# A later place for four key casts, and a third queue for seven stores, in a fused attention and GELU kernel

## The chip, the cores and the metric

The kernel runs on one core of one Trainium2 chip. The metric is the device time of one execution in microseconds (us); several executions are timed and the median counts. Engines are named as the profile names them: PE multiplies matrices (PEld loads its weights), DVE and ACT work on vectors, POOL (GpSimd) does too and issues DMAs, SP only issues DMAs; ACT can issue them as well.

## What is computed

The reference is sliding-window attention, window 32 to either side, for 8 batches, 8 heads, 576 positions and 64 elements a head, followed by a two-layer feed-forward with the tanh form of GELU on the 4608 rows that come out of it:

```python
scores = scale * np.matmul(q, k.transpose(0, 1, 3, 2))
mask = np.abs(pos[:, None] - pos[None, :]) <= window
attn = exp(where(mask, scores, -1e9) - max) / sum
x = (attn @ v).transpose(0, 2, 1, 3).reshape(4608, 512)
h = x @ w_in                        # 512 -> 2048
g = 0.5 * h * (1.0 + np.tanh(c * (h + 0.044715 * h * h * h)))
out = g @ w_out                     # 2048 -> 512
```

Inputs and output are float32.

## The kernel before

The 4608 rows are cut into nine tiles of 512 (t = 0 to 8; `NT` is 9). While the feed-forward of tile t runs on PE, the attention of batch b = t + 1 is worked in between its matmuls, and the raw data of batch t + 2 is loaded and cast. The heads of a batch go in pairs (g = 0 to 3), and the last positions of all pairs make a fifth group (g = 4). A group is scored on PE (`score`), exponentiated on ACT, masked on DVE (`mask`, line 511), summed by a matmul with ones (`sum_up`, line 516), weighed with V on PE (`times`, line 526), inverted on ACT (`invert`, lines 553 and 554) and written to the next rows on DVE (`spread`, line 563).

The order of instructions on each engine is the order of the program text; nothing reorders it. The last part of a tile is a loop over 112 steps, each with one product matmul of the output layer (`ffn_out`, line 774, its matmul on line 793). Before step i, everything that a plan lists under i is put out. A plan is a table from step to acts: `s` scores a group, `m` masks it, `g` sums and weighs a pair of groups, `x` spreads one, `a` casts a quarter of the next batch's queries (`turn_query`, cast on line 431), `b` casts a quarter of its keys (`turn_keys`, cast on line 441). The last query quarter issues a transposing DMA on SP (line 435), and every second key quarter issues one (line 443). Tiles 4 to 6 use `PLAN`, tile 3 `PLAN_L`; line 1024 chooses:

```python
PLAN = {7: "s0@0 s1@1 v-1", 16: "m0 m1 x-1", 35: "s2@0 g0@1", 38: "m2", 46: "x0 a0", 52: "x1 a1 a2 a3",
        63: "s3@0 s4@1", 66: "b0 b1", 70: "m3", 74: "m4", 80: "b2 b3", 88: "g2@1", 108: "x2", 112: "x3"}
```

The keys that `turn_keys` casts come from four DMAs a batch, issued by `load_qk` (line 204) on SP at the front of the same tile, after two transposing DMAs on SP (lines 426 and 451).

The output layer is a Strassen-like scheme of seven products (`WINO`, n = 0 to 6), 16 matmuls each. After each product's last matmul, in steps 15, 31, 47, 63, 79, 95 and in `ffn_last`, DVE (or ACT) copies or adds the result: line 816 after step 63, line 819 after step 79 (822 in the last tile), line 825 after step 95, line 834 at the end of the tile. The result tile is `yo`, and `store` (line 746) writes its rows to the output. A store of 128 rows is cut into pieces where the rows of the output are not contiguous, and the pieces go round the queues that the caller names; without any, they go to POOL's queue. The last tile names queues, as its stores end the program: SP for the left half of the first 256 rows, then SP and ACT in turn. DMAs of SP and ACT share eight semaphores in rotation, and an issue waits until the store that had its semaphore before has landed. At the end of the program (shown as line 1170 in the profile) every engine drains, SP waits for all semaphores of DMAs, and all engines meet at POOL.

Of the kernel before, what the change touches and what calls it, by code (L numbers as in the profile page):

```python
# [36 lines left out]
def cut(b):  # L37
    return 120 if b else 128
# [7 lines left out]
PLAN = {7: "s0@0 s1@1 v-1", 16: "m0 m1 x-1", 35: "s2@0 g0@1", 38: "m2", 46: "x0 a0", 52: "x1 a1 a2 a3",  # L46
        63: "s3@0 s4@1", 66: "b0 b1", 70: "m3", 74: "m4", 80: "b2 b3", 88: "g2@1", 108: "x2", 112: "x3"}
# [5 lines left out]
PLAN_0 = {4: "s0@0", 9: "r1@1", 14: "s1@0", 15: "w1", 16: "m0", 19: "k2", 22: "r2@1", 23: "m1", 28: "s2@0 w2",  # L53
# [15 lines left out]
PLAN_2 = {7: "s0@0 s1@1 v-1", 16: "m0 m1 x-1", 35: "s2@0 g0@1", 38: "m2", 46: "x0", 52: "x1",  # L69
          63: "s3@0 s4@1", 66: "a0 a1", 70: "m3", 74: "m4", 80: "a2 a3", 88: "g2@1", 108: "x2", 112: "x3"}  # L70

PLAN_L = {7: "s0@0 s1@1 v-1", 16: "m0 m1 x-1", 35: "s2@0 g0@1", 38: "m2", 46: "x0", 52: "x1",
          63: "s3@0 s4@1", 66: "a0 a1", 70: "m3", 74: "m4", 80: "a2 a3", 84: "b0", 88: "g2@1", 92: "b1", 95: "b2 b3", 108: "x2", 112: "x3"}

PLAN_1 = {12: "s0@0 s1@1 s2", 16: "m0 m1", 36: "m2", 56: "s-1@0 g0@1", 62: "m-1 x0", 64: "x1",
          80: "s3@0 g-1@1", 81: "m3", 90: "x2", 92: "x-1", 104: "v3 s4@1", 112: "x3 m4"}
# [6 lines left out]
LONE = 3  # L83
# [5 lines left out]
def kernel(  # L89
# [9 lines left out]
    nc = tc.nc  # L99
    B, H, S, D = q.shape  # L100
# [304 lines left out]
    def bank(i):  # L405

        return psM.tile([128, 512], FP32, name="mm", tag=f"x{i}")
# [206 lines left out]
    def in_w(eng, unit, *which):  # L614

        i, j = UNITS[unit] // 2, 2 * (UNITS[unit] % 2)
        A11, A12, A21, A22 = (w_cols[:, d:d + 2, c + i, j:j + 2, :] for c in (0, 2) for d in (0, 2))
        if (unit, "s") not in mixed:
            if unit == "A":
                wc = rawp.tile([128, 4, 2, 2, 128], FP16, name="wcA", tag="q0")  # L620
                mixed[unit, "s"] = [wc[:, x] for x in range(4)]
            else:
                mixed["xw"] = rawp.tile([128, 2, 4, 2, 256], FP16, name="xw", tag="k1")
                mixed[unit, "s"] = [mixed["xw"][:, 1, x].rearrange("p d (h c) -> p d h c", h=2) for x in range(4)]
        S1, S2, S3, S4 = mixed[unit, "s"]
        mixed[unit, "w"] = dict(A11=A11, A12=A12, A22=A22, S1=S1, S2=S2, S3=S3, S4=S4)
        for x in which:
            dst, a, b, op = ((S1, A21, A22, ALU.add), (S2, S1, A11, ALU.subtract),
                             (S3, A11, A21, ALU.subtract), (S4, A12, S2, ALU.subtract))[x - 1]
            eng.tensor_tensor(dst, a, b, op=op)  # L630
# [102 lines left out]
    def sums(t, i, which=slice(0, 4)):  # L733

        g, r = gTs[t], slice(2 * i, 2 * i + 2)
        A11, A21, A12, A22 = (g[:, r0 + 2 * i:r0 + 2 * i + 2, c:c + 256]
                              for r0 in (0, 8) for c in (0, 256))
        S1, S2, S3, S4 = (wino[f"S{n}"][:, r, :] for n in (1, 2, 3, 4))
        for dst, x, y, op in ((S1, A21, A22, ALU.add), (S2, S1, A11, ALU.subtract),
                              (S3, A11, A21, ALU.subtract), (S4, A12, S2, ALU.subtract))[which]:  # L740
            nc.vector.tensor_tensor(dst, x, y, op=op)  # L741
# [4 lines left out]
    def store(t, t4, yo, cols=slice(0, 512), *engs):  # L746

        m = i = 0
        while m < 128:
            b, c = divmod(t * 512 + t4 * 128 + m, S)  # L750
            q0, n = (0, cut(b)) if c < 4 * cut(b) else (cut(b), 144 - cut(b))
            j, p = divmod(c - 4 * q0, n)
            e = min(n - p, 128 - m)
            eng = engs[i % len(engs)] if engs else nc.gpsimd
            eng.dma_start(out_v[b, j, q0 + p:q0 + p + e, cols], yo[m:m + e, cols])  # L755
            m += e
            i += 1
# [16 lines left out]
    def ffn_out(t, i):  # L774

        n, blk, f = i // 16, i // 8 % 2, i % 8
        if n == 1 and t >= NT - 2:
            blk, f = divmod(i % 16, 4) if i % 16 < 8 else (i // 2 % 2, i // 4 % 4 * 2 + i % 2)
        a, w, new = WINO[n]
        end = t == NT - 1  # L780
        if i % 16 == 0 and new:
            pys[n % 2] = bank((1 + n) % 2)
            if end and n == 4:
                pys["apart"] = psO.tile([128, 512], FP32, name="py2", tag="O")
        py = pys[n % 2].rearrange("p (b c) -> p b c", b=2)
        apart = end and blk and n in (4, 6)
        if a[0] == "A":
            r0, c0 = 8 * (int(a[2]) - 1) + f, 256 * (int(a[1]) - 1) + 128 * blk
            lhsT = gTs[t][:, r0, c0:c0 + 128]
        else:  # L790
            lhsT = wino[a][:, f, 128 * blk:128 * blk + 128]
        one = end and n in (4, 6)
        nc.tensor.matmul(pys["apart"][:, 0:256] if apart else py[:, blk, :], lhsT,  # L793
                         wino[w][:, f, :], start=(new and i % (8 if one else 16) == 0),
                         stop=(i % (8 if one else 16) == (7 if one else 15)),
                         skip_group_check=True)
        if i % 16 < 15:
            return
        yo, left, right = wino["yo"], slice(0, 256), slice(256, 512)
        C11, C12, C21, C22 = (yo[:, r:r + 2, c] for r in (0, 2) for c in (left, right))  # L800

        M1, U2, U3 = C21, C12, C22
        if n == 0:
            (nc.scalar.copy if t >= NT - 2 else nc.vector.tensor_copy)(M1, py)
        elif n == 1:
            nc.vector.tensor_tensor(U2, py, M1, op=ALU.add)  # L806
        elif n == 2:
            nc.vector.tensor_copy(C11, py)
            if t >= NT - 2:
                for step in "z1 z2 z3".split():  # L810
                    sums(t, int(step[1]), PARTS[step[0]])
            if end:
                for x in range(2):
                    store(t, x, yo[:, x, :], left, nc.sync)
        elif n == 3:
            nc.vector.tensor_tensor(U3, py, M1, op=ALU.add)
        elif n == 4:
            if not end:
                nc.vector.tensor_tensor(C22, py, U3, op=ALU.add)
            else:  # L820
                for x, part in enumerate((py[:, 0, :], pys["apart"][:, 0:256])):
                    nc.vector.tensor_tensor(C22[:, x, :], part, U3[:, x, :], op=ALU.add)
                    store(t, 2 + x, yo[:, 2 + x, :], right, nc.sync, nc.scalar)
        elif n == 5:
            nc.vector.tensor_tensor(C21, py, M1, op=ALU.add)  # L825
            for x in range(2):
                store(t, 2 + x, yo[:, 2 + x, :], *((left, nc.sync, nc.scalar) if end else ()))

    def ffn_last(t):
        py = pys[0].rearrange("p (b c) -> p b c", b=2)  # L830
# [75 lines left out]
    s0 = psS.tile([128, 2, 512], FP32, name="ps_o", tag="S0")  # L906
# [4 lines left out]
    s1 = psS.tile([128, 2, 512], FP32, name="ps_o", tag="S1")  # L911
# [63 lines left out]
    for t in range(NT):  # L975
        b = t + 1
        att = b < B
        if t:
# [19 lines left out]
            for fc in range(begun, NF if t < LONE else 0):  # L998
# [22 lines left out]
                    pair_v(b, nc.vector.tensor_copy)  # L1021
                if t == LONE - 1 and fc in (8, 9, 10, 11):
                    in_w(nc.vector, "B", (8, 9, 10, 11).index(fc) + 1)
        plan = PLAN_0 if not t else PLAN_1 if t == 1 else PLAN_2 if t == LONE - 1 else PLAN_L if t == LONE else PLAN if att else {16: "v-1", 40: "x-1"} if t == B - 1 else {}

        def group(g):
            return (b, g) if g >= 0 else (b - 1, 4)
# [6 lines left out]
        for i in range(113 if t else 65):  # L1034
# [100 lines left out]
            if t == 0 and i < 64:  # L1135
                ffn_out_0(*ORDER_0[i])
            elif t and i < 112:
                ffn_out(t, i if t < NT - 1 or not 28 <= i < 36 else i + 4 if i < 32 else i - 4)
# [36 lines left out]
```

## Time and profile before

| what | value |
|---|---|
| timed executions | 292.73, 292.84, 294.62 us; median 292.84 |
| the profiled execution's own time | 293.94 us |
| its span, first to last instruction | 292.2 us |
| PE busy | 283.3 us, 97% |
| DVE, ACT, POOL busy | 77%, 67%, 32% |
| granted TensorE clock | 1.00 |
| tile 3, tile 4, tile 5, tile 6 (by PE's first matmul of each) | 30.22, 30.99, 29.88, 29.89 us |

The profile is one execution. Its own time is about 1.7 us more than its span, which is what lies before the first and after the last instruction. A line of the timeline gives start, duration, engine, line, operation, output and inputs with shapes, and in brackets how long the engine stood idle before and what ended that. In the table of stages each engine has its busy time and its number of instructions, and the last columns are the granted clock, the share of the DMA engines and GB/s. Landing times of DMAs are read from the semaphore updates that the trace holds.

### The profile page before, as it was taken

What the parts mean: (1) busy time and instruction counts of PE and PEld (TensorE: products, weight loads), DVE (VectorE), ACT (ScalarE), POOL (GpSimd) and SP (SyncE); (2) the same over time, 40 slices, a digit from 0 to 9 for tenths busy, and PEclk for the clock granted to TensorE, in tenths of its full rate; (3) what the DMA queues carried; (4) which work ended last, traced back from release to release, by engine and by line L of the source; (5) the groups of instructions that cost most, each with busy time, mean ns of one, the idle gap of its engine ahead of it and who ended that gap; (6) DMA issues with size and microseconds to landing.
All of it is one profiled execution on the core that took longest, in us unless ns stands there. A gap on an engine that the chain in (4) does not pass through costs nothing.

```text
span 292.2 us, 7443 instructions
## 1 busy us (share of the span) xinstructions
PE 283.3 (97%) x2993; PEld 197.0 (67%) x2993; DVE 225.5 (77%) x499; ACT 196.9 (67%) x323; POOL 92.7 (32%) x158
## 2 busy tenths in 40 slices
PE   8889999999999999999999989999999999999994
PEld 3535544557765677668866876688667877887783
DVE  4755377998897968798998778889888967875682
ACT  5875867878577865687658845895689577905800
POOL 3435324102318652505166108500800070016000
PEclk9999999999999999999999999999999999999999
DMA  7999998999999999869999998698820031005013
GB/s 219 276 372 399 358 311 201 246 195 187 272 222 195 261 217 192 220 156 217 134 185 248 179 162 185 193 180 126 186 45 2 2 87 61 0 3 144 0 43 103
DMA packets 113792, 51.01 MB, mean 175 GB/s; under 512 B 97839, under 2 KB 109615, under 8 KB 113502
## 3 DMA queue, kind: packets, MB, share of 16 engines
q1 hardware_dynamic: 89604, 38.77, 59.0%
q0 software_dynamic: 23088, 10.82, 23.1%
q10 hardware_dynamic: 1066, 0.96, 1.0%
q8 instruction: 23, 0.38, 0.6%
q14 instruction: 11, 0.09, 0.1%
HBM read 36.70 MB, written 9.44 MB: 158 GB/s over the span
## 4 chain that ended last, share of the span: by engine, by line
PE 82%; DMA 9%; SPq 5%; issue 1%; DVE 1%; POOL 0%; ACTq 0%; DVEq 0%
PE mm L793 29%; PE ph L600 17%; PE mm L600 14%; PE pu L656 7%; DMA kr<-in_k_dram 3%; PE ps_s L489 3%; PE py L765 3%; PE mm L765 2%; DMA wst<-in_moe_w_in_dram 2%; SPq L204 2%; DMA qr<-in_q_dram 2%; DMA V<-in_v_dram 1%; PE ps_od L516 1%; SPq L282 1%; PE ps_d L516 1%
## 5 line engine op out<-in xcount | busy, mean ns | idle before, releaser
L600 PEld LDWEIGHTS <-w_in 128*128 128x128 f16 x448 | 50.2, 113 | 39.6 <-POOL w_in L261 1.2
L755 POOL DMA_DIRECT2D out_dram<-y x77 | 42.0, 554 | 93.2 <-DVE y L825 75.3
L600 PE MATMUL ph<-xT,w_in 128*128 128x512 f16 x240 | 60.4, 379 | 0.6 <-POOL w_in L261 0.6
L793 PEld LDWEIGHTS <-s 128*128 128x128 f16 x512 | 49.4, 98 | 6.6 <-issue 0.4
L600 PE MATMUL mm<-xT,w_in 128*128 128x512 f16 x208 | 53.5, 379 | 0.0
L793 PE MATMUL mm<-t,s 128*128 128x256 f16 x376 | 44.9, 273 | 0.2 <-DVE y L806 0.2
L793 PEld LDWEIGHTS <-gT 128*128 128x128 f16 x384 | 36.2, 98 | 6.6 <-issue 0.3
L502 ACT ACTIVATE pe<-ps_s 128x960 f16<-128x960 f32 (+1 forms) x31 | 29.5, 974 | 14.2 <-PE ps_s L489 14.1
L793 PE MATMUL mm<-w_out,gT 128*128 128x256 f16 x256 | 32.6, 273 | 0.0
L741 DVE TENSOR_TENSOR s<-gT 128x512 f16<-128x512 f16 x64 | 26.9, 425 | 5.7 <-ACT gT L608 2.9
L608 ACT ACTIVATE gT<-mm 128x512 f16<-128x512 f32 x28 | 16.5, 599 | 21.6 <-PE mm L600 21.5
L608 ACT ACTIVATE gT<-ph 128x512 f16<-128x512 f32 x38 | 20.9, 606 | 6.6 <-PE ph L600 6.6
L114 ACT ACT_TABLE_LOAD x18 | 23.1, 1283 | 2.2 <-issue 1.9
L554 ACT ACTIVATE lt<-lt 128x480 f32<-128x480 f32 (+3 forms) x36 | 21.1, 585 | 1.1
L511 DVE TENSOR_TENSOR pe<-pe,band 128x960 f16<-128x960 f16 x28 | 18.1, 664 | 2.0 <-ACT pe L502 1.9
L704 ACT ACTIVATE gT<-ph 128x512 f16<-128x512 f32 x22 | 13.2, 600 | 4.8 <-PE ph L600 4.7
L793 PE MATMUL mm<-t,gT 128*128 128x256 f16 x128 | 16.2, 273 | 0.0
L526 PEld LDWEIGHTS <-V 128*64 128x64 f16 x520 | 12.6, 112 | 5.2 <-DVE V L237 1.3
L741 DVE TENSOR_TENSOR s<-s,gT 128x512 f16<-128x512 f16 x32 | 14.4, 450 | 1.1
L553 ACT ACTIVATE lt<-ps_od 128x480 f32<-128x480 f32 (+2 forms) x13 | 7.1, 546 | 11.6 <-PE ps_od L526 6.2
L793 PE MATMUL mm<-w_out,s 128*128 128x256 f16 x120 | 14.6, 273 | 0.0
L227 POOL DMA_DIRECT2D V<-in_v_dram x16 | 14.3, 912 | 0.5 <-PE mm L600 0.2
(153 smaller groups left out, 472.7 us busy)
## 6 DMA issues: line engine op xcount, KB each, us to landing
kr<-in_k_dram SPq DMA_DIRECT2D x31, 256.0 KB
qr<-in_q_dram SPq DMA_DIRECT2D x6, 1024.0 KB
wst<-in_moe_w_in_dram SPq DMA_DIRECT2D x8, 512.0 KB
vr<-in_v_dram SPq DMA_DIRECT2D x12, 256.0 KB
wst<-in_moe_w_out_dram SPq DMA_DIRECT2D x2, 1024.0 KB
wst<-in_moe_w_out_dram SPq DMA_DIRECT2D x4, 512.0 KB
V<-in_v_dram POOLq DMA_DIRECT2D x16, 128.0 KB, 8.2
qr<-in_q_dram SPq DMA_DIRECT2D x7, 256.0 KB
```

The costliest lines, as they stand in the source:

```text
L114: nc.scalar.add_instruction(mybir.InstLoadActFuncSet(name=nc.get_next_instruction_name(), act_func_set_id=which, ins=[], outs=[]))
L227: nc.gpsimd.dma_start(V[:, c, :, :], v[b, :, 128 * c:128 * c + 128, :].rearrange("h p d -> p h d"))
L502: nc.scalar.activation(pe, ps[:, :, 0:w], AF.Exp, scale=SCALE)
L511: nc.vector.tensor_tensor(pe, pe, m.rearrange("k (o j) p -> k o j p", o=1).broadcast_to(list(pe.shape)), op=ALU.mult)
L554: nc.scalar.activation(lt[:, 0:n], lt[:, 0:n], AF.Exp, scale=-1.0)
L600: nc.tensor.matmul(ph, w_cols[:, dc, fc // 4, fc % 4, :], xT[:, dc, t * 512 % RING:t * 512 % RING + 512], start=(dc == 0), stop=(dc == 3))
L608: nc.scalar.activation(gTs[t][:, fc, :], phs[fc], AF.Gelu_apprx_tanh)
L656: nc.tensor.matmul(ps[:, 256 * h:256 * h + 256], lhs[:, d, h, :], rhs[:, d, :], start=(n in (0, 2, 4) and h == d == 0), stop=(h == d == 1) ...
L741: nc.vector.tensor_tensor(dst, x, y, op=op)
L755: eng.dma_start(out_v[b, j, q0 + p:q0 + p + e, cols], yo[m:m + e, cols])
L765: nc.tensor.matmul(pys[t4], gTs[0][:, fc, t4 * 128:t4 * 128 + 128], w_out16[:, fc, :], start=new, stop=(fc == NF - 1))
L793: nc.tensor.matmul(pys["apart"][:, 0:256] if apart else py[:, blk, :], lhsT, wino[w][:, f, :], start=(new and i % (8 if one else 16) == 0) ...
```

## The change

Two edits. First, tile 4 (`LONE + 1`) gets a plan of its own, `PLAN_M`, in which the key casts b0, b1, b2 and b3 of batch 6 stand at steps 84, 92 and 95, after the masks m3 and m4 and after the addition that follows step 79; in `PLAN` they stand at 66 and 80. Everything else in the plan is the same. Second, in the last tile the stores that follow the addition after step 95 (line 825) go to other queues: the first 128 rows all to SP, the second 128 rows to ACT and POOL in turn; before, both went to SP and ACT in turn.

```diff
+PLAN_M = {7: "s0@0 s1@1 v-1", 16: "m0 m1 x-1", 35: "s2@0 g0@1", 38: "m2", 46: "x0 a0", 52: "x1 a1 a2 a3",
+          63: "s3@0 s4@1", 70: "m3", 74: "m4", 84: "b0", 88: "g2@1", 92: "b1", 95: "b2 b3", 108: "x2", 112: "x3"}
@@ ffn_out @@
         elif n == 5:
             nc.vector.tensor_tensor(C21, py, M1, op=ALU.add)
             for x in range(2):
-                store(t, 2 + x, yo[:, 2 + x, :], *((left, nc.sync, nc.scalar) if end else ()))
+                store(t, 2 + x, yo[:, 2 + x, :],
+                      *((left, *((nc.scalar, nc.gpsimd) if x else (nc.sync,))) if end else ()))
@@ the choice of the plan @@
-        plan = ... else PLAN_L if t == LONE else PLAN if att else ...
+        plan = ... else PLAN_L if t == LONE else PLAN_M if t == LONE + 1 else PLAN if att else ...
```

The pieces of the seven stores after line 825 were 40, 32, 24 and 24 rows on SP and 88, 24 and 24 on ACT; they are 40 and 88 on SP, 32, 24 and 24 on ACT and 24 and 24 on POOL.

More of the change, by code (lines that the diff above doesn't have):

```diff
@@ L1023 @@
                     in_w(nc.vector, "B", (8, 9, 10, 11).index(fc) + 1)
-        plan = PLAN_0 if not t else PLAN_1 if t == 1 else PLAN_2 if t == LONE - 1 else PLAN_L if t == LONE else PLAN if att else {16: "v-1", 40: "x-1"} if t == B - 1 else {}
+        plan = PLAN_0 if not t else PLAN_1 if t == 1 else PLAN_2 if t == LONE - 1 else PLAN_L if t == LONE else PLAN_M if t == LONE + 1 else PLAN if att else {16: "v-1", 40: "x-1"} if t == B - 1 else {}
         def group(g):
```

## The prediction

> **What bounds the kernel now.** I read the page's shares first: PE is busy 97% of the span at full granted clock, and the chain of work is 82% PE. So an edit pays only where PE stands still, or after its last matmul. Cutting the span into tiles, and tiles 4 and 5 at the same point of their own course (the score matmuls of groups 3 and 4, before step 63), gives four stages:
>
> ```profile
> 145.66:168.42 22.76, 22.76 (x230) 15.94 (x227) 19.49 (x46) 17.24 (x29) 10.79 (x17) 1.00 1.32 205
> 168.42:176.65 8.23, 7.33 (x115) 6.11 (x115) 6.75 (x17) 4.52 (x7) 0.73 (x2) 1.00 0.98 143
> 176.65:199.40 22.75, 22.75 (x229) 15.95 (x227) 19.34 (x44) 17.23 (x29) 9.95 (x16) 1.00 1.13 190
> 199.40:206.53 7.13, 7.13 (x115) 6.07 (x115) 6.52 (x15) 4.51 (x7) 0.73 (x2) 1.00 0.76 139
> ```
>
> Columns: window, its length, then PE, PEld, DVE, ACT and POOL busy. The first stages are equal (22.76 and 22.75 us). The second takes 8.23 us in tile 4 and 7.13 in tile 5, with the same 115 matmuls. So tile 4 loses 1.10 us there. The timeline shows how:
>
> ```profile
> 169.70 0.69 DVE L816 TENSOR_TENSOR y<-mm,y 128x512 f32<-128x512 f32 x1
> 171.68 0.76 DVE L441 CAST k<-kr 128x512 f16<-128x512 f32 x2 [1.30 <-DMA kr<-in_k_dram]
> 172.36 0.65 DVE L511 TENSOR_TENSOR pe<-pe,band 128x960 f16<-128x960 f16 x1
> 172.93 0.55 DVE L511 TENSOR_TENSOR pet<-pet,band 128x768 f16<-128x768 f16 x1
> 173.40 0.68 DVE L819 TENSOR_TENSOR y<-mm,y 128x512 f32<-128x512 f32 x1
> ...
> 171.77 0.39 PE L516 MATMUL ps_od<-pe,ones 128*64 128x480 f16 x2
> 173.06 0.39 PE L516 MATMUL ps_d<-pe,ones 128*64 128x480 f16 x2 [0.90 <-DVE pe L511]
> ```
>
> DVE works in order. At 170.38 it reaches batch 6's key casts (b0, b1), whose load lands at 171.56; it stands 1.30 us, the mask of group 3 comes that much late, and PE's denominator matmul waits 0.90 us for it. Tile 5 has the same order and no wait, because its last key load lands at 200.91 and its casts start at 201.15.
>
> At the end of the program I read the DMA queues and the shutdown (line 1170):
>
> ```profile
> 288.90 0.33 ACTq L755 DMA_DIRECT2D out_dram<-y  x1
> 289.26 0.32 SPq L755 DMA_DIRECT2D out_dram<-y  x1
> ...
> 261.98 5.77 POOL L755 DMA_DIRECT2D out_dram<-y  x11 [20.61 <-DVE y L825]
> L1170 POOLq DRAIN x3: 46/93/6027, 266.5 to 292.0; - x3
> L1170 SPq EVENT_SEMAPHORE  x11: 17/28/28, 289.6 to 292.2; - x11
> ```
>
> DVE's last addition ends at 288.32, the last store is issued on SP at 289.26 and lands at 290.89. SP then passes the remaining store semaphores one by one (about 0.06 us each, to 291.34), all engines meet at POOL at 291.50, and the span ends 0.73 us later. The reader should note POOL's first DRAIN: 6.03 us, 266.53 to 272.56, behind its last store, whose issue ended at 267.75 and which landed at 269.65. It ends 4.81 us after that issue and 2.91 us after that landing. Today 19 idle microseconds hide it.
>
> **The change, part 1: tile 4.** Nothing is added or removed: four casts (0.33 us apart) and their two key transposes move. b0 goes from step 66 to 84, b1 to 92, b2 and b3 from 80 to 95; in DVE's order masks m3, m4 and addition L819 (step 79) now precede all four casts, and the addition at step 95 (L825) follows them. Worked out: L816 at 169.70, m3 at 170.30, m4 at 170.87, L819 at 171.34, casts from 171.94. The load is there at 171.56, so the wait is gone with 0.38 us to spare. m3 ends at 170.95, before PE wants it (171.99), so PE runs as in tile 5. What is queued behind the casts: L825, which in tile 5's rhythm is due at 173.84 while the casts end near 173.3, so the load may land another 0.5 us late for nothing. The transposes on SP: the first follows the query transpose (issue ends 172.74) as now, the second follows at about 174.1 instead of 174.78; behind them on SP stands tile 5's query transpose, which waits for DVE until 180.43. Cost nil, while that gap of four microseconds lasts. No store, POOL step or PE order changes.
> Gain: at most 1.10 us (tile 5's stage). At the low end tile 5 gives some back: its casts had 0.24 us of slack, and they will be wanted 1.10 us sooner, at 200.05. If its load kept its clock time, m3 would end at 202.23 where PE wants it at 201.87: 0.36 lost, 0.74 left. But SP issues tile 5's loads after waits inside tile 5, so they should move with it. I take 1.10.
>
> **Part 2: the last tile's stores.** Addition L825 ends at 286.85. Its seven stores ran as SP 40, 32, 24, 24 rows and ACT 88, 24, 24; now SP 40 and 88, ACT 32, 24, 24, POOL 24 and 24. Behind them wait the four stores of line 834: SP 56 and 48 rows, ACT 72 and 80.
> SP: 40 at 286.88, 88 at 287.21, 56 at 287.58 (addition done 287.45), 48 at 288.37 (done 288.32), where it stood at 289.26; SP's one-landing-per-semaphore wait (it stood until 289.19 for an earlier ACT store) falls away, the semaphore it takes now having been free since 287.18. ACT: the first four as now, the fourth at 288.18; the 80 rows wait for the landing of ACT's first store, 88 rows (288.83) before, 32 now. SP's 40 rows issued at the same moment landed at 288.45, so between 288.45 and 288.83: the 80 rows are issued at 288.55 to 288.90, and land 1.82 us later, as they did. The last landing moves from 290.89 to between 290.38 and 290.73, and on a semaphore that SP asks eighth instead of second, which spares most of the 0.43 us of asking. SP's side would be done 0.53 to 0.88 us sooner; I take 0.85, since 32 rows are nearer to 40 than to 88.
> The Trainium skill ("DMA: Bandwidth & Descriptors", section "Issuing engines are not separate DMA queues") says that more issuing engines save only the sequencer's issue time; that would leave the same 0.53 to 0.88, and the trace agrees that the engines are not full there, 0.62 busy from 288.50 to 289.50.
> POOL: after DVE's L825 of tile 7 it took 0.30 us to its first store (261.68 to 261.98), each issue 0.53. So 287.15 and 287.67, ending 288.19, landing after 1.8 to 2.4 us as small stores there did: by 290.1. That alone is hidden. What is not: its DRAIN now stands behind these stores. The trace has one DRAIN behind stores. Counted from the last issue (4.81) it ends at 293.0; from the last landing (2.91), 292.4 to 293.0; if it grows with the number of stores (11 then, 2 now), 0.87 after the issue, 289.1, hidden; the other two, without stores, took 0.05 and 0.09. With 0.73 us of shutdown behind it, the span would end at 293.1 to 293.7 against 292.24, a loss of 0.9 to 1.5; hidden, a gain of 0.85. I take a loss of 1.3, by the only row of a DRAIN behind stores.
>
> **Sum.** The profiled execution took 293.94 us: span 292.24 and 1.70 around it. 293.94 - 1.10 + 1.3 = 294.1. That execution is 1.10 above the median shown (292.84), so the median frame gives 293.0.
>
> **Rivals.**
> A, the DRAIN is short: part 2 gains 0.85 instead of losing 1.3, and 292.84 - 1.95 = 290.9; with tile 4's low end, 291.3. For it: only two small stores, landed by 290.1. Against: the row above, where DRAIN outlasts the landing by 2.91. It decides if DRAIN ends before 290.6.
> The Trainium skill ("DMA: Bandwidth & Descriptors", section "Anatomy of one DMA") gives a POOL store about 2.0 us fixed; an estimate by that page alone has POOL done near 289.7 and the sum of A.
> B, slower: the key wait is not removed but comes back at tile 5's casts, which stay ahead of its masks. For it: 0.24 us of slack there, four key loads landing over 10 us on DMA engines that the window table shows full. It costs from 0.36 us (landing fixed in clock time) to the whole 1.10 when it lands 0.7 later still: 293.4 to 294.1. It decides once that landing follows tile 5's start by more than 24.5 us (24.26 now). The same time comes out if the timed runs, which spread over 1.9 us, have no wait in tile 4 to remove.
> C, neither DRAIN nor tile 4 counts: 292.84 - 0.85 = 292.0. It needs A's condition and B's together.
>
> **How the numbers follow.** Forecast (wait removed, DRAIN exposed) 0.47, its own range 292.6 to 293.6 (DRAIN by its two ends, tile 4 by 1.10 or 0.74); A 0.30; B 0.14; C 0.07; anything else 0.02. The range takes A's 290.9 and B's 294.1, since neither can be left out within 2 in 10; C lies inside. One per cent is 2.93 us, about what a measurement of this kernel can tell from no change; no case reaches it, so same 0.95, faster 0.02, slower 0.03.
>
> **What would show it.** Right: tile 4 as long as tile 5 (29.9), no wait of L441 on kr, no wait of L516 on L511; SP's last store near 1.1 us earlier against DVE's last addition; POOL's DRAIN ending 4 to 5 us after its last store's issue, and after SP is done. Wrong: a DRAIN that ends before SP is done (then A), a wait of L441 for kr in tile 5 (B), or a POOL store that lands after ACT's last.

## The result and the profile after

The changed kernel is slower by under half a per cent: median 295.12 us against 293.96 us, 22 executions each. The ratio, taken over the executions in the faster of the two states that this kernel shows and so not the quotient of these medians, is 1.0045, 95% interval 1.0023 to 1.0066, that is 1.3 us (0.7 to 1.9). The prediction had 293.0 us, 0.2 above the median that it knew, in a range of 290.9 to 294.1. It called anything under one per cent no change; 0.45% is under that, but the interval is clear of 1, and 295.12 is above the range. The median before over these 22 executions is also 1.1 us above that of the three that the prediction had.

| profiled executions | before | after |
|---|---|---|
| own time, span | 293.94, 292.24 | 294.71, 292.91 |
| tile 4 | 30.99 | 29.89 |
| DVE's last addition ends | 288.33 | 287.35 |
| last landing of SP's and ACT's stores | 290.89 | 289.70 |
| SP has asked all semaphores | 291.41 | 289.84 |
| POOL's DRAIN ends | 272.56 | 292.13 |
| from DVE's last addition to the end | 3.91 | 5.56 |

The work up to DVE's last addition became 0.98 us shorter and the rest 1.65 us longer. Both halves can be read in the trace. Lines of the changed kernel have numbers three to four higher than before. First its stages around tiles 4 and 5, cut as before (window, length, then busy time of PE, PEld, DVE, ACT, POOL):

```profile
145.78:168.53 22.75, 22.75 (x229) 15.93 (x227) 19.49 (x46) 17.24 (x29) 10.47 (x17) 1.00 1.29 210
168.53:175.66 7.13, 7.13 (x115) 6.07 (x115) 6.64 (x17) 4.50 (x7) 0.72 (x2) 1.00 0.91 118
...
198.42:205.55 7.13, 7.13 (x115) 6.13 (x115) 6.61 (x15) 4.51 (x7) 0.73 (x2) 1.00 0.72 129
```

Tile 4's second stage is now as long as tile 5's, 7.13 us, and PE is busy all of it. The timeline of DVE and PE there:

```profile
169.80 0.69 DVE L819 TENSOR_TENSOR y<-mm,y 128x512 f32<-128x512 f32 x1
170.40 0.66 DVE L514 TENSOR_TENSOR pe<-pe,band 128x960 f16<-128x960 f16 x1
170.97 0.56 DVE L514 TENSOR_TENSOR pet<-pet,band 128x768 f16<-128x768 f16 x1
171.44 0.69 DVE L822 TENSOR_TENSOR y<-mm,y 128x512 f32<-128x512 f32 x1
172.04 1.43 DVE L444 CAST k<-kr 128x512 f16<-128x512 f32 x4
173.95 0.69 DVE L828 TENSOR_TENSOR y<-mm,y 128x512 f32<-128x512 f32 x1 [0.49 <-PE mm L796]
...
171.88 0.39 PE L519 MATMUL ps_od<-pe,ones 128*64 128x480 f16 x2
172.10 0.37 PE L519 MATMUL ps_d<-pe,ones 128*64 128x480 f16 x2
```

No bracket there names kr any more, and the second denominator matmul follows the first without a wait. DVE even stands 0.49 us before L828, so here the casts cost nothing at their new place. The timeline at the end of the program:

```profile
286.16 1.00 POOL L758 DMA_DIRECT2D out_dram<-y  x2 [19.39 <-DVE y L828]
...
286.92 0.42 DVE L838 TENSOR_TENSOR y<-py,y 128x256 f32<-128x256 f32 x1 [0.45 <-PE py L796]
...
287.37 0.32 SPq L758 DMA_DIRECT2D out_dram<-y  x1
287.65 0.33 ACTq L758 DMA_DIRECT2D out_dram<-y  x1
```

And the shutdown's line among the groups by line (three DRAINs: shortest, median and longest in ns, then when the first and the last of them start):

```profile
L1174 POOLq DRAIN  x3: 46/93/5562, 286.6 to 292.6; - x3
```

SP's and ACT's last stores come right behind the addition. POOL's two stores are issued by 287.16 and land at 288.27 and 289.06. Its DRAIN, which before was 6.03 us long and hidden behind other work, is 5.56 us long, starts at 286.57 and ends at 292.13, 4.97 us behind POOL's last issue and 2.29 us after SP is done. All engines meet at POOL at 292.17. The chain of the page doesn't show this, since it follows the program's own instructions; the shutdown's line does.

### The profile page after: what moved, and what is told of

Same layout as the page of the kernel before. It is cut to its first block, busy times and chain, and to the rows that moved or that the text cites. A ratio compares the mean times of both kernels' runs of the same rounds, so it can differ in the third digit from the quotient of the medians.

```text
span 292.9 us, 7444 instructions
## 1 busy us (share of the span) xinstructions
PE 283.2 (97%) x2993; PEld 196.9 (67%) x2993; DVE 225.9 (77%) x499; ACT 196.7 (67%) x323; POOL 93.9 (32%) x160
## 4 chain that ended last, share of the span: by engine, by line
PE 82%; DMA 9%; POOL 3%; SPq 3%; issue 1%; DVE 0%; ACT 0%; ACTq 0%; DVEq 0%
PE mm L796 31%; PE ph L603 15%; PE mm L603 13%; PE pu L659 7%; PE ps_s L492 3%; DMA out_dram<-y 3%; DMA vr<-in_v_dram 3%; PE py L768 3%; PE mm L768 2%; DMA wst<-in_moe_w_in_dram 2%; POOL out_dram L758 2%; PE ps_od L519 2%; DMA qr<-in_q_dram 1%; SPq L285 1%; PE ps_o L529 1%; PE mm L659 1%
## 5 line engine op out<-in xcount | busy, mean ns | idle before, releaser
L758 POOL DMA_DIRECT2D out_dram<-y x79 | 42.9, 551 | 112.5 <-DVE y L828 94.0
L492 PEld LDWEIGHTS <-KT 64*64 64x64 f16 x576 | 10.0, 106 | 6.1 <-issue 4.0
```

What stands on the lines that cost most here:

```text
L492: nc.tensor.matmul(sides[h][64 * half:64 * half + 64, 4 * n * r:4 * n * r + 4 * n].rearrange("k (j p) -> k j p", j=4)[:, :, p0 - q0:p1 - q ...
```

## The experiments

The theory to start with: POOL's DRAIN behind the late stores ends the program. Rivals: the stores themselves are slow on POOL's queue; tile 4's gain is not in the timed executions; the new plan costs something elsewhere. The table has every run but e7 and e8, which are the kernel before again. Ratios are to the kernel before, with 95% intervals; "tail" is the time from DVE's last addition to the end of the span.

| kernel | ratio | tail | DRAIN ends after POOL's last work |
|---|---|---|---|
| e1_plan_only | 0.9972 (0.9938 to 1.0007) | 3.93 | 4.81 |
| e2_stores_only | 1.0062 (1.0029 to 1.0096) | 5.56 | 4.97 |
| e3_plan_two_queues | 0.9973 (0.9942 to 1.0003) | 3.90 | 4.81 |
| e4_pool_early | 0.9977 (0.9945 to 1.0010) | 3.54 | 4.97 |
| e5_late_pool_copy | 1.0002 (0.9961 to 1.0043) | 4.45 | 4.83 |
| e6_one_pool_store | 1.0007 (0.9971 to 1.0044) | 4.99 | 4.89 |
| e9_copy_early_drain | 0.9991 (0.9947 to 1.0034) | 3.90 | 0.07 |
| e10_stores_early_drain | 0.9996 (0.9956 to 1.0036) | 3.35 | 1.99 |
| e11_earlier_drain | 0.9938 (0.9905 to 0.9971) | 3.55 | 2.96 |
| e12_stores_early_drain_5 | 0.9956 (0.9927 to 0.9985) | 3.36 | 2.17 |

**The two edits apart.** e1_plan_only keeps the plan and puts the stores back:

```diff
-                store(t, 2 + x, yo[:, 2 + x, :],
-                      *((left, *((nc.scalar, nc.gpsimd) if x else (nc.sync,))) if end else ()))
+                store(t, 2 + x, yo[:, 2 + x, :], *((left, nc.sync, nc.scalar) if end else ()))
```

> Only the plan of tile 4 is changed; all stores as before. Theory (the wait of tile 4's key casts is in every execution, as in the profiled one): tile 4 takes 29.9 us in the profile, no wait of the key casts for their load, time 1.1 us under before (ratio 0.996). Rival 1 (the wait is in the profiled execution only, or in few): the profile the same, the time within 0.3 us of before. Rival 2 (the wait comes back at tile 5's casts): tile 5 longer than 29.9 us in the profile and the time 0 to 0.7 us under before.

Tiles 4 and 5 take 29.89 us each, no cast waits. The time is 0.8 us under before, though the interval just reaches no change. Rival 2 is out in this profile; rival 1 is taken up by e7 and e8.

e2_stores_only keeps the stores and puts tile 4 back:

```diff
-... else PLAN_M if t == LONE + 1 else PLAN if att ...
+... else PLAN if att ...
```

> Only the queues of the last tile's stores are changed; tile 4 has its old plan. Theory (POOL's DRAIN behind the late stores ends the program): in the profile the DRAIN ends 4.8 to 5.0 us after POOL's last store's issue and about 2.2 us after SP is done; the time is 1.7 us over before if the tail alone counts (ratio 1.006), so the whole change's 1.3 would be this less a small gain of tile 4. Rival (the stores themselves are slower on POOL's queue): the last store lands later than 2.6 us after DVE's last addition, which is where it landed before.

The time is 1.8 us over before. The DRAIN ends at 292.99, 2.24 us after SP is done (290.75). The last store landed 2.41 us after DVE's last addition (290.61 against 288.20), sooner than the 2.56 before, so the rival is out. The two edits multiply to 1.0034, which agrees with the whole, 1.0045, within the intervals.

**Without POOL, and with POOL early.** e3_plan_two_queues:

```diff
-                      *((left, *((nc.scalar, nc.gpsimd) if x else (nc.sync,))) if end else ()))
+                      *((left, *((nc.scalar, nc.sync) if x else (nc.sync,))) if end else ()))
```

> The new plan of tile 4, and the seven stores on SP (40, 88, 24, 24 rows) and ACT (32, 24, 24) with none on POOL. Theory (DRAIN): no late DRAIN, the tail from DVE's last addition to the end is 3.5 to 3.9 us again (3.9 before, 5.6 after), time like that of the new plan alone, 0 to 0.3 us better. Rival (the rest of the change's loss is elsewhere, in the plan): still about 1 us over before.

Tail 3.90, ratio that of the plan alone. So the change's loss comes with POOL's two stores.

e4_pool_early, from the plan alone:

```diff
                 for x in range(2):
-                    store(t, x, yo[:, x, :], left, nc.sync)
+                    store(t, x, yo[:, x, :], left, nc.gpsimd if x else nc.sync)
```

> The new plan of tile 4; the seven stores as before on SP and ACT, but two stores of the third product's result (48 and 80 rows, some 5 us earlier) go to POOL instead of SP. Theory (what counts is when POOL's last issue ends, plus about 4.9 us): the DRAIN ends near 287.5 in the profile, before SP is done, and the time is that of the new plan alone. Rival (any POOL store in the last tile costs, whenever it comes): 1 us or more over the new plan alone.

The DRAIN ended at 288.08, 3.1 us before SP was done (291.20), and the time is that of the plan alone. So POOL stores in the last tile cost nothing here when they come 5 us earlier. These two have 128 rows, the change's two 48, and the DRAIN is 4.97 us behind the last issue in both: the additional rows and bytes do not show in it.

**What the DRAIN waits for.** e5_late_pool_copy, from the two queues:

```diff
+            if end:
+                nc.gpsimd.tensor_copy(after, yo[:, 3, 0:1])
```

> As the kernel with two queues, and POOL copies one column of the result tile into a spare tile after DVE's addition of line 825, so POOL works as late as it did with its two stores but issues no DMA (the copy is extra work that no output reads). Theory (the long DRAIN belongs to DMAs that POOL issued): the DRAIN ends within 0.3 us of the copy, SP is the last to be done, the tail from DVE's last addition to the end is 3.9 us and the time that of the two queues, about 0.8 us under before. Rival (any late work on POOL makes its DRAIN some 5 us long): the tail is 5.5 us and the time 1 us or more over before.

Here my theory fell. No DMA was late on POOL, its last one had landed 17 us before the copy (268.21), and yet the timeline has, at the copy:

```profile
285.56 0.19 POOL L833 CAST after<-y 128x1 f16<-128x1 f32 x1 [19.22 <-DVE y L828]
```

and the shutdown's line:

```profile
L1176 POOLq DRAIN  x3: 46/93/5026, 285.6 to 291.1; - x3
```

A copy of 0.19 us, and a DRAIN of 5.03 that ends 4.83 us behind it, 0.6 us after SP is done. So a long DRAIN needs no late store that has yet to land; it followed POOL's last work, which was no DMA. The tail is 4.45 and not the 5.5 of the rival, since the copy ends 1.16 us before DVE's last addition does and the changed kernel's last issue 0.19.

e6_one_pool_store:

```diff
-                      *((left, *((nc.scalar, nc.gpsimd) if x else (nc.sync,))) if end else ()))
+                      *((left, *((nc.scalar, nc.gpsimd, nc.scalar, nc.sync, nc.scalar) if x else (nc.sync,))) if end else ()))
```

> As the changed kernel, but POOL has only the first of its two late stores; the other goes to SP. Theory (the DRAIN ends a fixed 4.9 us after POOL's last issue, whatever the number): the DRAIN ends 4.9 us after that issue, which is 0.5 us sooner, so the tail is 5.0 to 5.1 us and the time 1.2 us over that of the two queues. Rival (it grows with the number of stores behind it): about half, 2.5 us after the issue, hidden, and a tail of 3.5 to 3.9.

The DRAIN ends 4.89 us after that issue, tail 4.99. The length hardly hangs on the number of late stores (4.97 with two); a store less mainly starts it half a microsecond sooner. That left two theories, told apart by a DRAIN of POOL's own after tile 7's stores, where POOL stands idle for 19 us. e9_copy_early_drain, from e5:

```diff
             if t < NT - 1:
                 store(t, x, yo[:, x, :])
+                if t == NT - 2 and x:
+                    nc.gpsimd.drain()
```

> As the kernel with POOL's late copy and no late DMA, and POOL gets a DRAIN of its own right after its stores of tile 7, some 20 us before the end, where nobody waits for POOL. Theory A (the 4.8 us are put off from the DMAs that POOL issued, and the first DRAIN pays them): the early DRAIN takes some 5 us, the last one ends within 0.3 us of the copy, the tail from DVE's last addition to the end is 3.9 us instead of 4.45. Theory B (every DRAIN behind any work on POOL takes 4.8 us): both are long, the tail stays 4.45.

The line of the early DRAIN and the shutdown's:

```profile
L844 POOLq DRAIN  x1: 6027/6027/6027, 266.3 to 266.3; - x1
```

```profile
L1178 POOLq DRAIN  x3: 34/102/270, 286.7 to 291.7; - x3
```

The early one took 6.03 us, as the shutdown's did before the change, and the shutdown's first is now 0.27 long and ends 0.07 us after the copy. Theory A holds: something is put off, and the first DRAIN pays it.

e10_stores_early_drain is the changed kernel with the same two lines.

> The changed kernel (two late stores on POOL) with the same early DRAIN of POOL after tile 7's stores. Theory A with a price for each series of DMAs, and theory B: the last DRAIN is 4.9 us behind the last store again, tail 5.56 us, time as the changed kernel, 1.3 us over before. Theory C (only the first DRAIN of the program's body is long, whatever lies behind it): the last DRAIN is short, the tail 3.4 us, and this kernel is some 1.3 us under before, the fastest of all.

The tail of 3.35 is the shortest of all so far. A (one price for each series of DMAs) and B, which both expected 5.56 again, are out. The shutdown's DRAIN ends 1.99 us behind the second late store, 0.13 us after it landed, and before SP is done (290.15): short, though not nothing. The ratio, 0.9996, doesn't show the gain of 1.3 us that theory C expected, though its interval reaches it (0.9956). e12_stores_early_drain_5 is the same kernel with more executions, measured beside e11_earlier_drain:

```diff
-                if t == NT - 2 and x:
+                if t == NT - 4 and x:
```

> The changed kernel with POOL's extra DRAIN after the stores of tile 5 instead of tile 7, so that 81 of POOL's DMAs lie before it and 23 behind. If what DRAIN pays is a price for each DMA since the last DRAIN (0.08 us each, as 4.81, 4.89 and 4.97 us behind 102, 103 and 104 of them suggest), the extra one takes about 3.1 us behind its last issue and the last one at most 2.0; if it is one price whatever the number, the extra one takes 4.8 again and the last one 4.8 as well or short, as it was behind two. The time: short last DRAIN, 1.3 us under before (ratio 0.9955); long, 0.5 to 1 over.

> The changed kernel with the extra DRAIN after tile 7's stores, as before, with more rounds: its profile has a tail of 3.35 us against 3.91 before and no wait in tile 4, so it should be 0.5 + 0.8 = 1.3 us under before (ratio 0.9955); if the gains of the profile are not in the timed executions, 0.998 to 1.000.

e11's two DRAINs, its own and the shutdown's:

```profile
L842 POOLq DRAIN  x1: 5509/5509/5509, 210.8 to 210.8; - x1
```

```profile
L1176 POOLq DRAIN  x3: 46/93/3552, 287.6 to 291.7; - x3
```

Program and trace have 80 of POOL's DMAs ahead of the extra DRAIN and 24 behind it, not 81 and 23 as was expected. The extra one ends 4.38 us behind its last issue (80 DMAs), the last one 2.96 (24 DMAs), 1.0 us after the last landing and 0.2 after SP is done. It is neither one price nor 0.08 us each (3.1 and 2.0 were expected): it is longer behind more DMAs since the last DRAIN, but less than in proportion. The 80 include all 21 loads of V that POOL issues and the 24 are stores alone, so number and kind are not told apart here. e12's shutdown:

```profile
L1176 POOLq DRAIN  x3: 46/102/2742, 286.0 to 289.9; - x3
```

Both are faster than before, by about half a per cent, and than the change: 0.9956 (0.9927 to 0.9985) and 0.9938 (0.9905 to 0.9971). These two intervals and e10's overlap, so e11 is not shown to be better than e12. Nor is either shown to be faster than the two queues without POOL (e3, 0.9973); that the early DRAIN makes late stores on POOL better than none stands in the tail alone (3.36 against 3.90).

**How often tile 4 waits.** e7_before_look and e8_before_look are two more profiles of the kernel before, unchanged:

> The kernel before, unchanged: how long do tile 4's key casts wait in another execution? If the wait is the same in every execution, 1.3 us and tile 4 takes 31.0; if it comes and goes with the landing of the load, anything from 0 to 1.3 (0.40 in the kernel with only the stores changed).

> The kernel before, unchanged, once more: the same question as in the look before this one.

In e7 the casts did not wait at all and tile 4 took 29.89 us. In e8 they waited longest of all, on DVE's timeline:

```profile
172.62 0.76 DVE L441 CAST k<-kr 128x512 f16<-128x512 f32 x2 [2.21 <-DMA kr<-in_k_dram]
```

and tile 4 took 31.89. With the first profile (30.99) and e2 (30.08), the old plan loses 1.10, 0.19, 0 and 2.00 us, 0.82 on average. That agrees with e1's 0.8 (0.28% of 293.96), more closely than four profiles and e1's interval can vouch for. In the ten profiles with the new plan tile 4 took 29.89 each time, also in e6, where the casts waited 0.7 us at their new place.

The wait explains only part of how far executions lie apart. e7 had none and took 296.25 us, more than the other three. From the first matmul of tile 4's first layer to the end of DVE's last addition it is 141.73 or 141.74 us in all eleven profiles without a wait that PE felt (e7 and the ten), and 142.83, 141.93 and 143.74 in the three where PE did wait (before, e2, e8). But that first matmul comes at 145.50 before, 145.61 after and 148.88 in e7, from 144.93 to 148.88 over all profiles, and neither edit touches what lies ahead of it.

## Why the prediction was wrong, point by point

The mechanism forecast, wait removed and DRAIN exposed, is what happened. What failed are three sizes of the sum: the tail's loss (1.65 us for "I take a loss of 1.3"), tile 4's gain (0.82 on average for "I take 1.10"), and the base of "the median frame gives 293.0" (293.96 for 292.84).

- **Tile 4: the mechanism was right, the size off.** "I take 1.10" was one execution's loss, taken off the median of others as if each had it. It comes and goes, 0 to 2.00, and 0.82 on average. The order on DVE came out as worked out, to 0.1 us. The transposes and tile 5 cost nothing: tile 5's casts waited 0.28 us in the profile after, and the tile took 29.89, 29.88 before, so rival B did not happen.
- **The stores of SP and ACT: right.** SP was done 2.49 us after DVE's last addition instead of 3.08, a gain of 0.59; the bounds were 0.53 to 0.88, and I took 0.85. Most of the missing 0.26 is that ACT's last store took 2.05 us to land where I had 1.82. The sign "SP's last store near 1.1 us earlier" did not follow from my own times, which give 0.89 (289.26 against 288.37); 0.90 was measured.
- **POOL's DRAIN: exposed, as forecast, but mis-sized.** "I take a loss of 1.3" lay between two ways of counting, from the last landing and from the last issue. e5 shows a DRAIN of this length with no late landing; counted from POOL's last work the loss would have been the upper end, 1.5, and 1.65 was measured, because the DRAIN is 0.16 us longer behind two more DMAs (4.81, 4.89, 4.97 behind 102, 103, 104).
- **Rival A's reason was half right.** The DRAIN is longer behind more DMAs, but all since the last DRAIN count, not the last few. The Trainium skill's price for a POOL store, about 2.0 us ("DMA: Bandwidth & Descriptors", section "Anatomy of one DMA"), is near what the trace has (2.11 and 2.41 from issue to landing here). The end that the estimate by that page gave, 289.7, was wrong for POOL because the DRAIN is not in it.
- **The frame.** 292.84, the median of three executions, became 293.96 with 22. In the profiles the executions differ most ahead of tile 4, where the sum has no term; that this is what moved the median is not shown. The difference forecast, +0.2, became +1.3: 0.28 of it is tile 4 (0.82 for 1.10) and 0.35 the tail (1.65 for 1.3), which gives +0.83, within the interval's 0.7 to 1.9; the two edits measured apart give 1.0034, +1.0. What else there is of the 1.3 stays open. The measured time left the range because both the frame and the difference were too low, by 1.1 us each.

## What to carry to other kernels

Before a late store or copy goes to POOL because it is idle, look at its DRAIN in the shutdown: if POOL has issued DMAs (some 100 here), its last work has to end some 5 us before the other engines are done. Where POOL has idle time earlier, a DRAIN of its own there takes that time while nobody waits, and late work on POOL becomes cheap (from 1.0045 to 0.9996 and 0.9956 in two measurements here). Leaving POOL out at the end did as well within the intervals (0.9973). A stall on a DMA's landing seen in one profile is one draw: two more profiles of the same kernel gave 0 and 2.2 us for 1.3.

## What the runs showed of the hardware that was not expected

POOL's DRAIN is long if POOL issued DMAs since its last DRAIN, and here also when they had landed 17 us before. Counted from the end of POOL's last work it ended 0.07 us later with no DMA since the last DRAIN, 2.0 to 2.2 with 2 (0.13 after the landing in both), 2.96 with 24, 4.38 with 80, 4.81 to 4.83 with 102, 4.89 with 103 and 4.97 with 104. What POOL does in that time, no run shows. A copy that followed a DMA on POOL in the middle of the program started as the DMA's issue ended (101.63 us, in the profile before), so there the copy did not pay it. With POOL's last work 5.4 us before the end of DVE's last addition (e4, 104 DMAs) instead of 0.19, it was 4.97 again, so it is counted from POOL's own last work and not from the other engines.
